# Six stream slots, 41 resident weight granules and a stream in QKV alone, in a recurrent transformer kernel

## The chip, the cores and the metric

One NeuronCore of a Trainium2 chip runs the kernel. The metric is the device time in microseconds (us) of one execution; the granted clock is that of TensorE (PE), as a share of 2.4 GHz.

## What is computed

x is (1, 2048, 1024) in bf16. With xn = layernorm(x) the result is x + A(xn) + B(xn).

```python
# A: 64 segments of 32 rows, 8 memory rows, 32 heads of 128
for s in range(64):
    h = concat([mem, xs])                  # 40 rows
    q, k, v = h @ Wq, h @ Wk, h @ Wv       # each 1024 x 4096
    p = softmax(mask(q @ k.T * scale))
    o = (p @ v) @ Wo                       # 4096 x 1024
    mem = o[:8]; outs.append(o[8:])
# B: two routed rows
r = x @ w_r; idx = two largest of r
y = (silu(x[idx] @ w_gate) * (x[idx] @ w_up)) @ w_down * sigmoid(r[idx])
B = x + scatter_add(y at idx)
```

The new memory is needed before the next segment can start, so the 64 segments run one after the other.

## The kernel before

The weights of A do not fit in SBUF. They are cut into 64 **granules** of 512 KB (128 x 2048 bf16): 48 for QKV, in six phases of eight (Q half 0, K half 0, Q half 1, K half 1, V half 0, V half 1; `PHASES`), and 16 for Wo, numbered 48 to 63. `N_RES` = 42 stay resident (`wres`, loaded at L107 in the prologue). The other 22 are fetched again in every segment, through a ring of `N_SLOT` = 4 tiles (pool `wstream`, tiles `g`): `fetch()` issues the next on SP's DMA queue (L248), `take` hands it out, and `used(g)` issues another fetch once PE has been given the matmuls of a streamed granule. So three fetches run ahead, in a fixed order. Before, the streamed granules are 16 of QKV (1, 4, 7, 10, 13, 16, 18, 21, ... 45) and six of Wo (48, 50, 53, 56, 59, 62).

The program has three parts. The **prologue** loads x, computes layernorm and writes its transposes to DRAM (`xT_d`, `zT_d`, `stl_d`), while the residents come in. The **expert stage** computes B for the two routed rows, with 46 fetches of w_gate, w_up and w_down through the same ring (L243, L245), and writes the two changed columns to `zT_d` (L318, SP's queue). The memory rows of `A_mem0` are then loaded on SP's queue (L368), transposed on PE and copied into `ST` (`mem_to_st`, L354 and L355). The **segment loop** (L374) runs, for each segment: the QKV matmuls (L505, result `PSm`); transposes of Q and K (L408); `scores(half)`, which adds the mask on PE and does the softmax on DVE and ACT over PSUM tile `SPS` (L448 max, L449 subtract, L451 exp into SBUF tile `EX`, L453 sum, then the products `PM` and `PL`); `attend` (L481, L483); the Wo projection (L545, `WO`); the output copy `OB`, and `mem_to_st` for the next segment.

The eight rows that the memory displaces in each segment ("left" rows, tile `STL`) are handled for four segments at once; with j = s mod 4, their V comes in the V phases of j=0 (L509, L530), Q in j=1, K in j=2, and their Wo projection (`WL`) in j=3. ACT's queue carries the small loads and stores (`ZT`, `ST`, `STL`, `QKL`, `qkl_d`, outputs). Order on each engine is as written; nothing reorders it.

Of the kernel before, what the change touches and what calls it, by code (L numbers as in the profile page):

```python
# [8 lines left out]
BF16 = mybir.dt.bfloat16  # L9
F32 = mybir.dt.float32  # L10
U32 = mybir.dt.uint32
ALU = mybir.AluOpType
ACTF = mybir.ActivationFunctionType
AX = mybir.AxisListType
PSUM = bass.MemoryType.PSUM
DRAM = bass.MemoryType.DRAM

N_RES = 42
N_SLOT = 4
NEG = -30000.0  # L20

PHASES = [(0, 0), (1, 0), (0, 1), (1, 1), (2, 0), (2, 1)]
# [3 lines left out]
def kernel(  # L26
# [16 lines left out]
    nc = tc.nc  # L43
    P = 128
# [3 lines left out]
    SEG = int(A_seg_len)  # L48
# [5 lines left out]
    KC = D // P  # L54
    FC = F // P
    SCALE = float(E) ** -0.5
    XM = SEG - M
    XL = M
    NK = M + SEG
# [8 lines left out]

    NG = 64
    n_str = NG - N_RES  # L70
    streamed = set(((2 * i + 1) * NG) // (2 * n_str) for i in range(n_str))

    def granule_dram(g):
        if g < 48:
# [10 lines left out]
    const = ctx.enter_context(tc.tile_pool(name="const", bufs=1))  # L85
    dram = ctx.enter_context(tc.tile_pool(name="dram", bufs=1, space=DRAM))
    wstream = ctx.enter_context(tc.tile_pool(name="wstream", bufs=N_SLOT))
    psA = ctx.enter_context(tc.tile_pool(name="psA", bufs=2, space=PSUM))
    psL = ctx.enter_context(tc.tile_pool(name="psL", bufs=1, space=PSUM))
    psT = ctx.enter_context(tc.tile_pool(name="psT", bufs=2, space=PSUM))  # L90
# [19 lines left out]
    IDENT = const.tile([P, P], BF16, name="IDENT")  # L110
    make_identity(nc, IDENT[:, :])
    MASK = const.tile([P, 2 * NK], BF16, name="MASK")
    PL = [const.tile([P, 4, 2, 32], BF16, name=f"PL{i}") for i in range(2)]
    for i in range(2):
        nc.gpsimd.memset(PL[i][:, :, :, :], 0.0)
    SPS = psS.tile([P, 4, 2, NK], F32, name="SPS")
    nc.vector.memset(SPS[:, :, :, :], 0.0)


    pc = ExitStack()  # L120
    pro = pc.enter_context(tc.tile_pool(name="pro", bufs=2))
    pro1 = pc.enter_context(tc.tile_pool(name="pro1", bufs=1))

    MF = pro1.tile([P, 2 * NK], F32, name="MF")
    nc.vector.memset(MF[:, :], 0.0)

    for q0 in range(0, P, 32):
# [3 lines left out]
    nc.vector.tensor_copy(out=MASK[:, :], in_=MF[:, :])  # L131

    RROW = wstream.tile([P, 2048], BF16, tag="g", name="RROW")[0:1, 0:S]
    WRT = pro1.tile([P, KC], BF16, name="WRT")
    nc.sync.dma_start(out=WRT[:, :], in_=B_w_r.rearrange("(k p) -> p k", p=P))
    V8 = const.tile([1, 8], F32, name="V8")
    I8 = const.tile([1, 8], U32, name="I8")
# [5 lines left out]
    def load_x(u):  # L143
        if 2 * u < NT:
            XP[u] = wstream.tile([P, 2048], BF16, tag="g", name="XP")
            nc.sync.dma_start(out=XP[u].rearrange("p (a d) -> p a d", a=2),
                              in_=x2[2 * u * P:(2 * u + 2) * P, :].rearrange("(a p) d -> p a d", a=2))
# [53 lines left out]
                          in_=Zt.rearrange("p s k r -> p s (k r)"))  # L201
        nc.sync.dma_start(out=stl_d[t][:, :], in_=L.rearrange("p k s r -> p (k s r)"))

    load_x(0)
    load_x(1)
    for t in range(NT + 4):
        if t < NT:
            if t % 2 == 1:
                load_x(t // 2 + 2)
            ST8[t] = ln_stats(pro, xt(t), P)  # L210
        if 0 <= t - 4:
            ln_e(t - 4)
        load_resident(2)
        if 0 <= t - 1 < NT:
            ln_b(t - 1)
        if 0 <= t - 2 < NT:
            ln_c(t - 2)
        if 0 <= t - 3 < NT:
            ln_d(t - 3)
# [5 lines left out]

    pc = ExitStack()
    pro = pc.enter_context(tc.tile_pool(name="prob", bufs=1))


    FH = F // 2  # L230
# [24 lines left out]

    for _ in range(N_SLOT - 1):
        fetch()
    XS = pro.tile([2, D], BF16, name="XS")
    vals = []
    for c in range(2):  # L260
# [56 lines left out]
    for c in range(2):  # L317
        nc.sync.dma_start(out=zT_d[bass.ds(vals[c] >> 5, 1), :, :, bass.ds(vals[c] & 31, 1)].rearrange("s p k r -> p (s k) r"),  # L318
                          in_=ZNEW[:, :, c:c + 1])
    pc.close()  # L320


    stp = ctx.enter_context(tc.tile_pool(name="stp", bufs=2, reuse_waits="tile"))
    one = ctx.enter_context(tc.tile_pool(name="one", bufs=1, reuse_waits="tile"))
    two = ctx.enter_context(tc.tile_pool(name="two", bufs=2, reuse_waits="tile"))

    def granule(g):
        return take("w", g) if g in streamed else res_tiles[g]

    def used(g):  # L330
        if g in streamed:
            fetch()

    def load_st(s):
        ST = stp.tile([P, KC, SEG], BF16, tag="st", name="ST")
        nc.scalar.dma_start(out=ST.rearrange("p k r -> p (k r)"), in_=xT_d[s // 4][s % 4])
        return ST

    def load_stl(g):
        STL = one.tile([P, KC, SEG], BF16, tag="stl", name="STL")  # L340
# [7 lines left out]
                                in_=qkl_d[s // 4][:, :, :, s % 4, :].rearrange("m h p c -> p (m h) c"))  # L348
        return t

    def mem_to_st(OB, ST):
        PTm = psT.tile([P, 2, P], BF16, tag="t", name="PTm")
        for c in range(2):
            nc.tensor.transpose(out=PTm[:, c, :], in_=OB[:, c * P:(c + 1) * P], identity=IDENT[:, :])  # L354
        nc.vector.tensor_copy(out=ST.rearrange("p (g c) r -> p c g r", c=2)[:, :, :, XM:SEG],  # L355
                              in_=PTm.rearrange("p c (g r) -> p c g r", g=4)[:, :, :, XM:SEG])

    def residual(PS, Zt):

        for g in range(4):  # L360
# [1 line left out]
                nc.tensor.matmul(PS[32 * g:32 * g + 32, c * P:(c + 1) * P], lhsT=Zt[:, 2 * g + c, :], rhs=IDENT[:, :],  # L362
                                 start=(c == 0), stop=False, tile_position=(0, 32 * g), skip_group_check=True)

    OB = two.tile([P, 256], BF16, tag="ob", name="OB")
    nc.vector.memset(OB[:, :], 0.0)
    for g in range(4):
        nc.sync.dma_start(out=OB[32 * g + XM:32 * g + SEG, :], in_=A_mem0[0, :, 256 * g:256 * (g + 1)])  # L368
    ST = load_st(0)
    STL = load_stl(0)  # L370
    QKL = load_qkl(0)
    mem_to_st(OB, ST)

    for s in range(NSEG):  # L374
        G, j = divmod(s, 4)
# [53 lines left out]
        def scores(half):  # L429
            if s == 0:  # L430
                for m in range(2):
                    nc.scalar.dma_start(out=QKL[:, m, half, :], in_=qkl_d[0][m, half, :, 0, :])
            q, k = QT[half], KT[half]
            nc.gpsimd.tensor_copy(out=k[:, :, 32:NK], in_=QKL[:, 1, half, :].rearrange("p (h r) -> p h r", r=XL))
            for il in range(4):
                for jq in range(4):
                    hh = 4 * il + jq
                    nc.tensor.matmul(SPS[32 * jq:32 * jq + 32, il, 0, :], lhsT=q[:, hh, :], rhs=k[:, hh, :],
                                     start=(il == 0), stop=True, tile_position=(0, 32 * jq), skip_group_check=True)
                    nc.tensor.matmul(SPS[32 * jq:32 * jq + XL, il, 1, :], lhsT=QKL[:, 0, half, hh * XL:(hh + 1) * XL],  # L440
                                     rhs=k[:, hh, :], start=False, stop=True, tile_position=(0, 32 * jq),
                                     skip_group_check=True)
            nc.tensor.matmul(SPS.rearrange("p i a k -> p i (a k)"), lhsT=IDENT[:, :],  # L443
                             rhs=MASK[:, :].unsqueeze(1).to_broadcast([P, 4, 2 * NK]),
                             start=False, stop=True, skip_group_check=True)
            S8 = SPS.rearrange("p i a k -> p (i a) k")
            NM = two.tile([P, 8], F32, tag="nm", name="NM")
            nc.vector.tensor_reduce(out=NM[:, :], in_=S8, axis=AX.X, op=ALU.max, negate=True)  # L448
            nc.vector.tensor_tensor(out=S8, in0=S8, in1=NM[:, :].unsqueeze(2).to_broadcast([P, 8, NK]), op=ALU.add)  # L449
            EX = one.tile([P, 8, NK], BF16, tag="ex", name="EX")  # L450
            nc.scalar.activation(out=EX[:, :, :], in_=S8, func=ACTF.Exp, scale=SCALE)  # L451
            DN = two.tile([P, 8], F32, tag="dn", name="DN")
            nc.vector.tensor_reduce(out=DN[:, :], in_=EX[:, :, :], axis=AX.X, op=ALU.add)  # L453
            nc.vector.reciprocal(out=DN[:, :], in_=DN[:, :])
            PM = one.tile([P, 8, 32], BF16, tag="pm", name="PM")
            PLt = PL[half].rearrange("p i a k -> p (i a) k")
            jp = (j + 3) % 4
            nc.gpsimd.memset(PLt[:, :, XL * jp:XL * (jp + 1)], 0.0)
            dnb = DN[:, :].unsqueeze(2)
            nc.vector.tensor_tensor(out=PM[:, :, :], in0=EX[:, :, 0:32], in1=dnb.to_broadcast([P, 8, 32]), op=ALU.mult)  # L460
            nc.vector.tensor_tensor(out=PLt[:, :, XL * j:XL * (j + 1)], in0=EX[:, :, 32:NK],
                                    in1=dnb.to_broadcast([P, 8, XL]), op=ALU.mult)
            PTm = two.tile([P, 4, 64], BF16, tag="ptm", name="PTM")
            PTl = two.tile([P, 4, 64], BF16, tag="ptl", name="PTL")
            nc.vector.transpose(out=PTm.rearrange("p i q -> p (i q)"), in_=PM.rearrange("p b k -> p (b k)"))
            nc.vector.transpose(out=PTl.rearrange("p i q -> p (i q)"), in_=PLt.rearrange("p b k -> p (b k)"))
            PTs[half] = (PTm, PTl)
            if half == 1 and s + 1 < NSEG:
                nxt["qkl"] = load_qkl(s + 1)

        def attend(half, ph):
            if half not in OT:
                OT[half] = two.tile([P, 4, 4, SEG], BF16, tag="ot", name="OT")
            PTm, PTl = PTs[half]
            OP = psO.tile([P, 2, 512], F32, tag="otp", name="OP")
            for il in range(4):
# [102 lines left out]
        for w, Gv in late[4:]:  # L579
            project(WL, w, Gv, lhs_left, w == late[-1][0])  # L580
        if j == 3:
            OL = one.tile([P, 256], BF16, tag="ol", name="OL")
            nc.scalar.copy(out=OL[:, :], in_=WL[:, 0:256])
            o4 = out2[4 * G * SEG:4 * (G + 1) * SEG, :].rearrange("(s r) d -> s r d", s=4)
            for g in range(4):
                nc.scalar.dma_start(out=o4[:, XM:SEG, 256 * g:256 * (g + 1)], in_=OL[32 * g:32 * (g + 1), :])
# [37 lines left out]
```

## Time and profile before

| | |
|---|---|
| runs | median 2810.72 us of 3 (2807.4 to 2813.32) |
| the profiled execution | 2811.76 us, its span 2810.0 us, mean granted clock 0.864 |
| busy share of the span | PE 69%, PE weight loads 36%, DVE 26%, ACT 16%, POOL 4% |
| chain that ended last | DMA 47%, PE 22%, issue 19%, DVE 7% |
| HBM read over the span | 804.28 MB |

The busy shares are averages over the three parts. The chain follows the work back from the last instruction; "issue" in it is time in which an engine waited for nothing that the profile shows. A wait is put down to what ended it. DMA share is the mean busy share of the core's 16 DMA engines; GB/s is what they moved.

### The profile page before, as it was taken

What the parts mean: (1) busy time and instruction counts of PE and PEld (TensorE: products, weight loads), DVE (VectorE), ACT (ScalarE), POOL (GpSimd) and SP (SyncE); (2) the same over time, 40 slices, a digit from 0 to 9 for tenths busy, and PEclk for the clock granted to TensorE, in tenths of its full rate; (3) what the DMA queues carried; (4) which work ended last, traced back from release to release, by engine and by line L of the source; (5) the groups of instructions that cost most, each with busy time, mean ns of one, the idle gap of its engine ahead of it and who ended that gap; (6) DMA issues with size and microseconds to landing.
All of it is one profiled execution on the core that took longest, in us unless ns stands there. A gap on an engine that the chain in (4) does not pass through costs nothing.

```text
span 2810.0 us, 82148 instructions
## 1 busy us (share of the span) xinstructions
PE 1949.7 (69%) x36873; PEld 998.7 (36%) x36873; DVE 722.0 (26%) x2021; ACT 459.1 (16%) x1017; POOL 112.9 (4%) x436
## 2 busy tenths in 40 slices
PE   3356777677777777767776777777677777777776
PEld 3222333333334333333333333333333333333333
DVE  4301222222222222222222222212222222222222
ACT  3201111111111111111111111111111111111111
POOL 4100000000000000000000000000000000000000
PEclk9668888889898898888988888988988888888888
DMA  9975988989898998979988898988889897988987
GB/s 299 318 265 179 311 299 293 300 279 336 292 318 300 310 316 275 312 268 319 298 301 300 279 306 286 317 302 300 295 298 314 280 318 268 309 301 293 316 304 264
DMA packets 367877, 831.69 MB, mean 296 GB/s; under 512 B 68482, under 2 KB 121762, under 8 KB 367524
## 3 DMA queue, kind: packets, MB, share of 16 engines
q1 hardware_dynamic: 292212, 796.00, 82.7%
q10 hardware_dynamic: 75312, 30.44, 4.0%
q8 instruction: 288, 4.72, 0.7%
q14 instruction: 65, 0.53, 0.1%
HBM read 804.28 MB, written 22.02 MB: 294 GB/s over the span
## 4 chain that ended last, share of the span: by engine, by line
DMA 47%; PE 22%; issue 19%; DVE 7%; ACT 2%; ACTq 1%; POOL 1%; SPq 1%; POOLq 0%; DVEq 0%
DMA g<-in_A_Wq_dram 14%; DMA g<-in_A_Wo_dram 13%; PE PSm L505 10%; DMA g<-in_A_Wv_dram 7%; DMA g<-in_A_Wk_dram 5%; PE WO L545 4%; DMA out_dram<-OB 2%; PE PSl L509 2%; DMA zT_d<-Tz 1%; PE PTq L408 1%; DMA qkl_d<-QS 1%; DVE SPS L449 1%; DVE NM L448 1%; ACT EX L451 1%; DVE DN L453 1%
## 5 line engine op out<-in xcount | busy, mean ns | idle before, releaser
L505 PE MATMUL PSm<-wres,ST 128*32 128x512 bf16 x8192 | 806.3, 436 | 14.7 <-DVE ST L355 13.9
L505 PE MATMUL PSm<-g,ST 128*32 128x512 bf16 x4096 | 454.0, 432 | 333.8 <-DMA g<-in_A_Wq_dram 186.8
L505 PEld LDWEIGHTS <-ST 128*32 128x32 bf16 x12288 | 332.1, 102 | 790.3 <-issue 459.6
L545 PEld LDWEIGHTS <-OT 128*32 128x32 bf16 x8192 | 233.7, 107 | 178.9 <-issue 153.6
L509 PE MATMUL PSl<-wres,STL 128*32 128x512 bf16 x2048 | 233.5, 443 | 50.3 <-DVE VL L530 47.0
L545 PE MATMUL WO<-g,OT 128*32 128x256 bf16 x3072 | 178.0, 313 | 121.6 <-DMA g<-in_A_Wo_dram 120.4
L517 ACT CAST XB<-PSm 128x512 bf16<-128x512 f32 x256 | 149.5, 584 | 654.9 <-PE PSm L505 475.5
L545 PE MATMUL WO<-wres,OT 128*32 128x256 bf16 x5120 | 254.3, 305 | 0.0
L486 ACT CAST OT<-OP 128x256 bf16<-128x256 f32 x256 | 95.2, 372 | 481.7 <-PE OP L483 481.7
L488 DVE CAST OTL<-OP 128x64 bf16<-128x64 f32 x256 | 57.5, 225 | 402.1 <-ACT OT L486 402.1
L408 PE MATMUL PTq<-IDENT,XB 128*128 128x128 bf16 x1024 | 108.4, 232 | 74.8 <-ACT XB L517 73.0
L448 DVE TENSOR_REDUCE NM<-SPS 128x8 f32<-128x320 f32 x128 | 62.9, 492 | 366.3 <-PE SPS L443 366.3
L451 ACT ACTIVATE EX<-SPS 128x320 bf16<-128x320 f32 x128 | 55.9, 437 | 612.1 <-DVE SPS L449 576.6
L509 PEld LDWEIGHTS <-STL 128*32 128x32 bf16 x3072 | 93.7, 107 | 143.9 <-issue 101.6
L416 DVE COPY KT<-PTq 128x512 bf16<-128x512 bf16 x128 | 54.3, 425 | 332.0 <-PE PTq L408 330.8
L408 PEld LDWEIGHTS <-XB 128*128 128x128 bf16 x1024 | 61.8, 102 | 203.0 <-ACT XB L517 172.2
L481 PE MATMUL OP<-PTM,VM 32*128 32x40 bf16 x2048 | 102.0, 186 | 42.5 <-DVE VM L527 38.2
L413 DVE COPY QT<-PTq 128x512 bf16<-128x512 bf16 x128 | 52.2, 408 | 272.6 <-PE PTq L408 272.6
L481 PEld LDWEIGHTS <-VM 32*128 32x128 bf16 x2048 | 70.1, 95 | 142.9 <-issue 92.9
L509 PE MATMUL PSl<-g,STL 128*32 128x512 bf16 x1024 | 113.9, 431 | 7.1 <-DVE XBl L521 7.1
L398 POOL COPY ZL<-ZT 128x64 bf16<-128x64 bf16 x64 | 15.1, 236 | 2424.7 <-DMA ZT<-zT_d 2246.7
L483 PE MATMUL OP<-PTL,VL 32*128 32x40 bf16 x2048 | 98.1, 182 | 0.0
(98 smaller groups left out, 1562.9 us busy)
## 6 DMA issues: line engine op xcount, KB each, us to landing
g<-in_A_Wq_dram SPq DMA_DIRECT2D x384, 512.0 KB
g<-in_A_Wo_dram SPq DMA_DIRECT2D x384, 512.0 KB
g<-in_A_Wk_dram SPq DMA_DIRECT2D x320, 512.0 KB
g<-in_A_Wv_dram SPq DMA_DIRECT2D x320, 512.0 KB
qkl_d<-QS ACTq DMA_DIRECT2D x64, 128.0 KB
QKL<-qkl_d ACTq DMA_DIRECT2D x63, 128.0 KB
g<-in_B_w_gate_dram SPq DMA_DIRECT2D x16, 448.0 KB
g<-in_B_w_up_dram SPq DMA_DIRECT2D x16, 448.0 KB
```

Source lines behind the costliest of these rows:

```text
L408: nc.tensor.transpose(out=PTq[:, il, :, :].rearrange("p j r -> p (j r)"), in_=XB[:, il * P:(il + 1) * P], identity=IDENT[:, :])
L416: nc.vector.tensor_copy(out=KT[half][:, :, 0:32], in_=pv)
L448: nc.vector.tensor_reduce(out=NM[:, :], in_=S8, axis=AX.X, op=ALU.max, negate=True)
L451: nc.scalar.activation(out=EX[:, :, :], in_=S8, func=ACTF.Exp, scale=SCALE)
L481: nc.tensor.matmul(o, lhsT=VM[q0:q0 + 32, c0:c0 + P], rhs=PTm[q0:q0 + 32, il, 0:NK], start=True, stop=False, tile_position=(q0, 0), skip_g ...
L483: nc.tensor.matmul(o, lhsT=VL[q0:q0 + 32, c0:c0 + P], rhs=PTl[q0:q0 + 32, il, 0:NK], start=False, stop=True, tile_position=(q0, 0), skip_g ...
L486: nc.scalar.copy(out=OT[half][:, 2 * ph:2 * ph + 2, :, :], in_=ov[:, :, :, 0:SEG])
L488: nc.vector.tensor_copy(out=OTL[:, h0:h0 + 8, j, :].rearrange("p (a i) r -> p a i r", a=2), in_=ov[:, :, :, SEG:NK])
L505: nc.tensor.matmul(PSm[32 * jq:32 * jq + 32, :], lhsT=ST[:, kc, :], rhs=Gv[:, 512 * jq:512 * (jq + 1)], start=(kc == 0), stop=(kc == KC - ...
L509: nc.tensor.matmul(PSl[32 * jq:32 * jq + 32, :], lhsT=STL[:, kc, :], rhs=Gv[:, 512 * jq:512 * (jq + 1)], start=(kc == 0), stop=(kc == KC - 1),
L517: nc.scalar.copy(out=XB[:, :], in_=PSm[:, :])
L545: nc.tensor.matmul(PS[32 * g:32 * g + 32, 0:256], lhsT=lhs(h), rhs=Gv[:, D * hs + 256 * g:D * hs + 256 * (g + 1)], start=False, stop=(last ...
```

## The change

- `N_SLOT` goes from 4 to 6 and `N_RES` from 42 to 41. The 23 streamed granules are spread over the first 48 granules only: 1, 3, 5, ... 21, 24, 26, ... 46. No Wo granule is streamed, so in j=3 all 16 `WL` projections are "late": four before `mem_to_st`, twelve after.
- The memory rows are loaded on ACT's queue ahead of the expert stage, and `ST` of segment 0 is made there too.
- Working tiles share buffers: `OT` with `QT` and `KT`, `PT2` of half 1 with `XB`, `OL` with `OB`, `MF` with a stream slot; `PL` lies in pool `one`. x is loaded three pairs ahead in place of two.
- The exponential is written back to `SPS` in PSUM; sum and products read it there.

```diff
-N_RES = 42
-N_SLOT = 4
+N_RES = 41
+N_SLOT = 6
...
-    streamed = set(((2 * i + 1) * NG) // (2 * n_str) for i in range(n_str))
+    streamed = set(((2 * i + 1) * 48) // (2 * n_str) for i in range(n_str))
...
-    load_x(0)
-    load_x(1)
+    for u in range(3):
+        load_x(u)
...
+    OB = pro.tile([P, 256], BF16, name="MEM0")
+    nc.vector.memset(OB[:, :], 0.0)
+    for g in range(4):
+        nc.scalar.dma_start(out=OB[32 * g + XM:32 * g + SEG, :], in_=A_mem0[0, :, 256 * g:256 * (g + 1)])
...
+    ST = load_st(0)
+    mem_to_st(OB, ST)
...
-    OB = two.tile([P, 256], BF16, tag="ob", name="OB")
-    nc.vector.memset(OB[:, :], 0.0)
-    for g in range(4):
-        nc.sync.dma_start(out=OB[32 * g + XM:32 * g + SEG, :], in_=A_mem0[0, :, 256 * g:256 * (g + 1)])
-    ST = load_st(0)
     STL = load_stl(0)
     QKL = load_qkl(0)
-    mem_to_st(OB, ST)
...
-            EX = one.tile([P, 8, NK], BF16, tag="ex", name="EX")
-            nc.scalar.activation(out=EX[:, :, :], in_=S8, func=ACTF.Exp, scale=SCALE)
+            nc.scalar.activation(out=S8, in_=S8, func=ACTF.Exp, scale=SCALE)
...
-            nc.vector.tensor_reduce(out=DN[:, :], in_=EX[:, :, :], axis=AX.X, op=ALU.add)
+            nc.vector.tensor_reduce(out=DN[:, :], in_=S8, axis=AX.X, op=ALU.add)
...
-            PTm = two.tile([P, 4, 64], BF16, tag="ptm", name="PTM")
-            PTl = two.tile([P, 4, 64], BF16, tag="ptl", name="PTL")
+            PT2 = one.tile([P, 2, 4, 64], BF16, tag="pt", name="PT2") if half == 0 else \
+                two.tile([P, 2, 4, 64], BF16, tag="xb", name="PT2")
+            PTm, PTl = PT2[:, 0], PT2[:, 1]
...
-                OT[half] = two.tile([P, 4, 4, SEG], BF16, tag="ot", name="OT")
+                OT[half] = one.tile([P, 4, 4, SEG], BF16, tag=("qt", "kt")[half], name="OT")
...
-            OL = one.tile([P, 256], BF16, tag="ol", name="OL")
+            OL = two.tile([P, 256], BF16, tag="ob", name="OL")
```

SP's queue between Q half 1 of one segment and K half 0 of the next, before (`g` is a tile of the ring):

```order
L248 DMA g<-in_A_Wq_dram 128x2048 x3
L248 DMA g<-in_A_Wk_dram 128x2048 x3
L248 DMA g<-in_A_Wv_dram 128x2048 x5
L248 DMA g<-in_A_Wo_dram 128x2x1024 x6
L248 DMA g<-in_A_Wq_dram 128x2048 x3
L248 DMA g<-in_A_Wk_dram 128x2048 x2
```

and after:

```order
L249 DMA g<-in_A_Wq_dram 128x2048 x3
L249 DMA g<-in_A_Wk_dram 128x2048 x4
L249 DMA g<-in_A_Wv_dram 128x2048 x8
L249 DMA g<-in_A_Wq_dram 128x2048 x4
L249 DMA g<-in_A_Wk_dram 128x2048 x4
```

The six Wo rows are gone, and seven more fetches stand in the QKV phases, three of them in V.

SP's queue behind the expert stage's last fetch, before (`ZNEW` holds the two changed columns):

```order
L318 DMA zT_d<-ZNEW 1024x1x1
L318 ISA
L318 REGISTER_ALU
L318 ISA
L318 DMA zT_d<-ZNEW 1024x1x1
L368 DMA OB<-in_A_mem_dram 8x256 x4
L248 DMA g<-in_A_Wk_dram 128x2048
```

and after:

```order
L333 DMA zT_d<-ZNEW 1024x1x1
L333 ISA
L333 REGISTER_ALU
L333 ISA
L333 DMA zT_d<-ZNEW 1024x1x1
L249 DMA g<-in_A_Wk_dram 128x2048 x2
```

The four loads of the memory rows no longer stand behind the two writes.

PE from the last transposes of the expert stage to the first matmul of the loop, before (`RNEW` holds the two changed rows):

```order
L314 LDWEIGHTS RNEW
L314 MATMUL PZ<-IDENT,RNEW 128x2
L354 LDWEIGHTS OB
L354 MATMUL PTm<-IDENT,OB 128x128
L354 LDWEIGHTS OB
L354 MATMUL PTm<-IDENT,OB 128x128
L505 LDWEIGHTS ST
L505 MATMUL PSm<-wres_207,ST 32x512
```

After, the two transposes of the memory rows stand ahead of the expert stage's first PE work:

```order
L267 LDWEIGHTS MEM_1142
L267 MATMUL PTm<-IDENT,MEM_1142 128x128
L267 LDWEIGHTS MEM_1142
L267 MATMUL PTm<-IDENT,MEM_1142 128x128
L284 LDWEIGHTS SIGR
L284 MATMUL PSG<-ONE_1187,SIGR 2x1
```

With them gone, the first L505 follows the last transpose of `RNEW` directly.

## Rows read from the trace of the kernel before

**Rows 1.** Head of the page: the span on core 0.

```profile
span 2810.0 us, 82148 instructions
```

**Rows 2.** Waits of the whole span: engine, form <- releaser: us, count, longest us.

```profile
PE PSm L505 <- DMA g<-in_A_Wq_dram: 186.8, 185, 3.0
PE WO L545 <- DMA g<-in_A_Wo_dram: 120.4, 165, 3.4
PE PSm L505 <- DMA g<-in_A_Wv_dram: 107.2, 102, 3.4
```

**Rows 3.** Windows: stretch us, busy by engine (x), granted clock, DMA share, GB/s.

```profile
110.00:118.00 8.00, 0.16 (x1) 0.07 (x1) 0.66 (x3) 2.77 (x3) 0.00 (x0) 0.50 1.00 386
140.00:160.00 20.00, 7.51 (x204) 6.37 (x202) 0.00 (x0) 0.00 (x0) 0.00 (x0) 0.50 0.96 336
118.30:122.30 4.00, 0.77 (x24) 0.79 (x25) 2.02 (x7) 2.42 (x3) 0.00 (x0) 0.50 0.03 13
1161.50:1181.10 19.60, 14.18 (x279) 7.16 (x282) 7.94 (x23) 3.42 (x8) 0.38 (x2) 0.85 0.96 321
1223.20:1226.20 3.00, 3.00 (x120) 2.48 (x116) 0.98 (x3) 1.20 (x4) 0.00 (x0) 1.00 0.61 200
1229.20:1232.60 3.40, 2.74 (x42) 1.53 (x34) 0.48 (x2) 0.27 (x1) 0.00 (x0) 0.50 1.03 408
1275.00:1305.00 30.00, 23.08 (x396) 10.32 (x399) 10.17 (x27) 5.66 (x12) 1.08 (x6) 0.93 0.93 308
270.50:2803.50 2533.00, 1826.23 (x35282) 922.19 (x35282) 651.55 (x1853) 401.97 (x924) 68.30 (x378) 0.87 0.88 300
```

**Rows 4.** DMA from 400 to 2700 us: queue: packets, MB, share.

```profile
DMA packets 291154, 688.16 MB, mean 299 GB/s; under 512 B 56025, under 2 KB 86764, under 8 KB 290849
q1 hardware_dynamic: 224123, 656.71, 83.1%
```

**Rows 5.** PE timeline: start us, us, operation [idle before]; loop's start and end.

```profile
190.36 0.35 PE L314 MATMUL PZ<-IDENT,RNEW 2*128 2x2 bf16 x8 [2.62 <-DVE RNEW L310]
199.86 0.37 PE L354 MATMUL PTm<-IDENT,OB 128*128 128x128 bf16 x2 [9.15 <-DMA OB<-in_A_mem_dram]
200.51 0.62 PE L505 MATMUL PSm<-wres,ST 128*32 128x512 bf16 x4 [0.28 <-DVE ST L355]
...
270.56 0.62 PE L505 MATMUL PSm<-wres,ST 128*32 128x512 bf16 x4 [0.28 <-DVE ST L355]
...
2800.92 2.54 PE L545 MATMUL WL<-wres,OTL 128*32 128x256 bf16 x80
```

**Rows 6.** PE timeline, a j=0 segment: granules 33, 46, Wo 59, next 1.

```profile
1209.01 0.40 PE L505 MATMUL PSm<-g,ST 128*32 128x512 bf16 x4 [1.57 <-DMA g<-in_A_Wv_dram]
...
1222.29 0.40 PE L505 MATMUL PSm<-wres,ST 128*32 128x512 bf16 x4
...
1228.99 0.62 PE L545 MATMUL WO<-g,OT 128*32 128x256 bf16 x8 [2.28 <-DMA g<-in_A_Wo_dram]
...
1233.45 0.64 PE L505 MATMUL PSm<-g,ST 128*32 128x512 bf16 x4
```

**Rows 7.** PE timeline, a j=3 segment: granule 46, two Wo stops, next 1.

```profile
1177.84 1.04 PE L505 MATMUL PSm<-wres,ST 128*32 128x512 bf16 x8
...
1184.81 0.40 PE L545 MATMUL WO<-g,OT 128*32 128x256 bf16 x8 [0.24 <-DMA g<-in_A_Wo_dram]
...
1186.56 0.40 PE L545 MATMUL WO<-g,OT 128*32 128x256 bf16 x8 [0.43 <-DMA g<-in_A_Wo_dram]
...
1189.95 0.39 PE L505 MATMUL PSm<-g,ST 128*32 128x512 bf16 x4
```

**Rows 8.** Chain that ended last, 118 to 136 us: start us, us, what.

```profile
122.44 3.57 DMA g<-in_B_w_gate_dram
```

**Rows 9.** Groups of DVE instructions: busy, mean ns, idle before.

```profile
L448 DVE TENSOR_REDUCE NM<-SPS 128x8 f32<-128x320 f32 x128 | 62.9, 492 | 366.3 <-PE SPS L443 366.3
L453 DVE TENSOR_REDUCE DN<-EX 128x8 f32<-128x320 bf16 x128 | 62.2, 486 | 75.9 <-ACT EX L451 75.9
```

More of the change, by code (lines that the diff above doesn't have):

```diff
@@ L87 @@
     wstream = ctx.enter_context(tc.tile_pool(name="wstream", bufs=N_SLOT))
+    stp = ctx.enter_context(tc.tile_pool(name="stp", bufs=2))
     psA = ctx.enter_context(tc.tile_pool(name="psA", bufs=2, space=PSUM))
@@ L112 @@
     MASK = const.tile([P, 2 * NK], BF16, name="MASK")
-    PL = [const.tile([P, 4, 2, 32], BF16, name=f"PL{i}") for i in range(2)]
-    for i in range(2):
-        nc.gpsimd.memset(PL[i][:, :, :, :], 0.0)
     SPS = psS.tile([P, 4, 2, NK], F32, name="SPS")
@@ L121 @@
     pro = pc.enter_context(tc.tile_pool(name="pro", bufs=2))
-    pro1 = pc.enter_context(tc.tile_pool(name="pro1", bufs=1))
-    MF = pro1.tile([P, 2 * NK], F32, name="MF")
+    MF = wstream.tile([P, 2 * NK], F32, tag="g", name="MF")
     nc.vector.memset(MF[:, :], 0.0)
@@ L133 @@
     RROW = wstream.tile([P, 2048], BF16, tag="g", name="RROW")[0:1, 0:S]
-    WRT = pro1.tile([P, KC], BF16, name="WRT")
+    WRT = const.tile([P, KC], BF16, name="WRT")
     nc.sync.dma_start(out=WRT[:, :], in_=B_w_r.rearrange("(k p) -> p k", p=P))
@@ L208 @@
             if t % 2 == 1:
-                load_x(t // 2 + 2)
+                load_x(t // 2 + 3)
             ST8[t] = ln_stats(pro, xt(t), P)
@@ L257, with load_st, mem_to_st @@
         fetch()
+    def load_st(s):
+        ST = stp.tile([P, KC, SEG], BF16, tag="st", name="ST")
+        nc.scalar.dma_start(out=ST.rearrange("p k r -> p (k r)"), in_=xT_d[s // 4][s % 4])
+        return ST
+    def mem_to_st(OB, ST):
+        PTm = psT.tile([P, 2, P], BF16, tag="t", name="PTm")
+        for c in range(2):
+            nc.tensor.transpose(out=PTm[:, c, :], in_=OB[:, c * P:(c + 1) * P], identity=IDENT[:, :])
+        nc.vector.tensor_copy(out=ST.rearrange("p (g c) r -> p c g r", c=2)[:, :, :, XM:SEG],
+                              in_=PTm.rearrange("p c (g r) -> p c g r", g=4)[:, :, :, XM:SEG])
+    ST = load_st(0)
+    mem_to_st(OB, ST)
     XS = pro.tile([2, D], BF16, name="XS")
@@ L320 @@
     pc.close()
-    stp = ctx.enter_context(tc.tile_pool(name="stp", bufs=2, reuse_waits="tile"))
     one = ctx.enter_context(tc.tile_pool(name="one", bufs=1, reuse_waits="tile"))
     two = ctx.enter_context(tc.tile_pool(name="two", bufs=2, reuse_waits="tile"))
+    PL = [one.tile([P, 4, 2, 32], BF16, name=f"PL{i}") for i in range(2)]
+    for i in range(2):
+        nc.gpsimd.memset(PL[i][:, :, :, :], 0.0)
     def granule(g):
@@ L332, in used @@
             fetch()
[L334 to L337, printed above, removed]
     def load_stl(g):
@@ L349, in load_qkl @@
         return t
[L351 to L356, printed above, removed]
     def residual(PS, Zt):
@@ L459, in scores @@
             dnb = DN[:, :].unsqueeze(2)
-            nc.vector.tensor_tensor(out=PM[:, :, :], in0=EX[:, :, 0:32], in1=dnb.to_broadcast([P, 8, 32]), op=ALU.mult)
-            nc.vector.tensor_tensor(out=PLt[:, :, XL * j:XL * (j + 1)], in0=EX[:, :, 32:NK],
+            nc.vector.tensor_tensor(out=PM[:, :, :], in0=S8[:, :, 0:32], in1=dnb.to_broadcast([P, 8, 32]), op=ALU.mult)
+            nc.vector.tensor_tensor(out=PLt[:, :, XL * j:XL * (j + 1)], in0=S8[:, :, 32:NK],
                                     in1=dnb.to_broadcast([P, 8, XL]), op=ALU.mult)
-            PTm = two.tile([P, 4, 64], BF16, tag="ptm", name="PTM")
-            PTl = two.tile([P, 4, 64], BF16, tag="ptl", name="PTL")
+            PT2 = one.tile([P, 2, 4, 64], BF16, tag="pt", name="PT2") if half == 0 else \
+                two.tile([P, 2, 4, 64], BF16, tag="xb", name="PT2")
+            PTm, PTl = PT2[:, 0], PT2[:, 1]
             nc.vector.transpose(out=PTm.rearrange("p i q -> p (i q)"), in_=PM.rearrange("p b k -> p (b k)"))
```

## The prediction

> **What bounds the kernel now.** I read the page's head first: one core, a span of 2810.0 us in an execution of 2811.76 us [rows 1]. Then the table of waits: the three largest groups of PE waits on a streamed granule add up to 186.8 + 120.4 + 107.2 = 414.4 us [rows 2], 6.5 us for each of 64 segments; 120.4 of it lies in the output projection, the rest in QKV.
>
> The windows tell whether this is a lack of rate or of slots [rows 3]. In the whole loop DMA is busy for 0.88 of the time at 300 GB/s; in the QKV phases of a j=3 segment 0.96 at 321 GB/s. So there the stream itself is nearly full; what is missing lies elsewhere. The stream queue q1 carries 656.71 of 688.16 MB [rows 4], a share of 0.954; at 321 GB/s one granule of 0.5243 MB therefore lands every 0.5243 / (0.954 x 0.321) = **1.71 us**. I call this spacing p.
>
> Before, a segment takes (2800.92 + 2.54 - 270.56) / 63 = 40.2 us [rows 5], the first, longer one left out.
>
> **The loop after the change.** A segment now streams 23 granules in place of 22, all in QKV (1, 3, ... 46), and none in Wo. I follow the PE from the moment it takes granule 1 (time 0) to granule 1 of the next segment.
>
> (a) With six slots, five fetches run ahead. Between granule 46 and the next granule 1 PE takes nothing from the stream, and the six slots fill at their own pace (6 x 1.71 = 10.3 us). Without waits this stretch lasts 1233.45 - 1222.29 - 2.28 = 8.88 us in a j=0 segment [rows 6], and I take that for j=0, 1 and 2; after a j=3 segment 1189.95 - 1177.84 - 0.24 - 0.43 = 11.44 us [rows 7]. The 2.28, 0.24 and 0.43 are the waits on streamed Wo in these rows, which the change removes.
>
> (b) The slot of granule 1 is free after its 0.40 us on PE [rows 6], and a transfer with nothing ahead of it takes 3.57 us from issue to landing [rows 8]: the 7th granule lands at 4.0 us, little after the six before it.
>
> (c) Sixteen more follow at p, if PE takes each at once: granule 46 lands at 4.0 + 16 x 1.71 = 31.4 us.
>
> (d) The cycle is 31.4 + 8.88 = 40.2 us for j=1 and j=2, and 31.4 + 11.44 = 42.8 us for j=3. For j=0 the V phases hold twice the PE work (the displaced rows): the first V granule, the 16th of the stream, lands at 4.0 + 9 x 1.71 = 19.4 us, and from the first streamed V to the next granule 1 PE needs 1233.45 - 1209.01 - 2.28 = 22.2 us [rows 6], together 41.6 us. The mean is (41.6 + 2 x 40.2 + 42.8) / 4 = **41.2 us**, 1.0 more than before, times 63 = **+63 us**.
>
> The price p is the unknown: no row shows six loop granules in flight. Its lower bound is 0.5243 / (0.954 x 0.408) = 1.35 us, from 3.4 us in a Wo phase after the stream had stood; 0.386 gives 1.42 us (seven or eight transfers in flight, PE nearly idle), and 0.5243 / 0.336 = 1.56 us is the expert stage, with four slots and no other queue at work. The upper bound, from the QKV phases of a j=2 segment with displaced K rows, is 0.5243 / (0.954 x 0.308) = 1.78 us [rows 3]. I take 1.71, since its row is the same phases with the same other traffic and DMA was busy for 0.96 of it, which seems to leave more slots 4% to fill. Each 0.1 us of p costs (9 + 3 x 16) / 4 x 0.1 = 1.43 us a segment, 90 us in all.
>
> **The start.** The memory rows came over SP's queue behind the two writes of zT_d, and PE stood from 190.71 (190.36 + 0.35) to 200.51, 9.15 of it put down to that load [rows 5]. They now come over ACT's queue before the expert stage and the two transposes go with them; SP keeps the two zT_d writes but has four fewer DMAs behind them. Taken: -9.7 us (200.51 - 190.71 = 9.80, less 0.1 for issue). The other end is 0, if a first-segment tile that reuses the expert stage's memory waits for those writes instead. Before the expert stage DMA is busy for 0.03 of 4 us while the routed rows are prepared [rows 3]; two more gate fetches of 0.459 MB now run there: -2 x 0.459 / 0.336 = -2.7 us (other end 0). One resident less: -0.524 / 0.386 = -1.4 us [rows 3] (other end 0, if the layer norm sets the end). Four small ACT-queue loads and x loaded one pair earlier are hidden by that same resident stream. Sum -13.8 us. The first segment stays as it is.
>
> **What I cost at nothing.** Softmax in PSUM: the sum over 320 f32 elements from PSUM takes about what the same reduction of bf16 from SBUF takes now (492 against 486 ns [rows 9]); SPS is held through sum and products too, but the next scores come 16 granules later. Bounds +-0.1 us a segment; cover: PE works on V meanwhile. Shared buffers: OT takes QT's and KT's buffer after the scores that read them, PT2 of half 1 that of an XB already transposed, OL that of an OB long sent; PE's own order covers each. In j=3, six projections of displaced rows move from before the memory transposes to after them, on the same engine: the sum is the same. SP's queue only holds fetches in the loop, so a fetch that waits delays none but fetches.
>
> **Sum.** 2811.76 + 63 - 13.8 = 2861 us for the profiled execution. The median of the runs stands 1.0 us below it, so the forecast is **2860 us**.
>
> **The rivals.**
>
> *A, six in flight raise the rate* (faster). If p falls to 1.56: j=0 takes 18.0 + 22.2 = 40.2, j=1 and 2 4.0 + 25.0 + 8.9 = 37.8, j=3 40.4, mean 39.1; (39.1 - 40.2) x 63 - 14 = -83 us, **2727 us**. It decides below p = 1.66, where the loop costs the 14 us that the start gives. For it: 386 GB/s with more transfers in flight and 408 in a Wo phase [rows 3], both with DMA busy throughout, while 0.96 stood beside 321 GB/s: a busy share near 1 is not yet the full rate. Against: the 408 was a burst, and the QKV phases carry the writes of ACT's queue besides. At p = 1.42 the mean would be 37.1 us and the time 2600 us. The Trainium skill's page "DMA: Bandwidth & Descriptors", section "Anatomy of one DMA", says that a transfer costs about 2.0 us plus its bytes over 436 GB/s and that the fixed part is mostly waiting for completion; what only waits can be covered by more transfers in flight, which speaks for A. By its fit a lone granule takes an estimated 3.2 us, against 3.57 us in the row for a gate transfer, which is smaller [rows 8]. The same page's section "Specifications" gives the core some 358 GB/s of HBM, by which p would be an estimated 1.54 us and the time some 2710 us; as a ceiling the 386 GB/s of this trace disagree with it.
>
> *B, the QKV phases fall to the lower rate* (slower still). The stream is denser there, and every write of ACT's queue meets it. At p = 1.78: 42.2, 41.4, 41.4 and 43.9, mean 42.2; +126 - 14, **2923 us**. For it: 308 GB/s in j=2. Against: that row also holds PE-side stops.
>
> *C, Wo without stops shortens the gap.* After the 2.28 us stop a matmul group takes 0.62 to 0.64 us where it took 0.40 before [rows 6]: the granted clock is 0.50 there, 1.2 GHz, and 1.00 before the stop [rows 3]. If that goes with the stop, about 1 us falls away in three of four segments: -47 us, **2813 us**, about no change. Against: PE then waits in QKV, and the clock may fall there as well.
>
> *D, the change doesn't reach the loop* (the streams' place doesn't matter, the bytes do): 23 granules in place of 22 at 300 GB/s in all give 40.2 x (0.954 x 23/22 + 0.046) = 42.0 us, which is near B.
>
> **How the numbers follow.** My forecast has 0.46, A 0.32, B with D 0.13, C 0.09. A measurement tells a change from none at about 0.2%, some 6 us. The forecast's own range, p from 1.66 to 1.76, is 2815 to 2905. The range of 8 in 10 takes in A at 1.56 and B without the start's gain: **2725 to 2940**. Faster by over 0.2%: A and a little of C, 0.35. Within 0.2%: most of C, 0.06. Slower: 0.59.
>
> **What would show it.** Right: no wait on Wo granules any more; the DMA share falling towards the end of each Wo phase; the PE's waits gathered in phases Q to V, most in the V phases; about 306 GB/s of stream there; the first segment starting near 187 us; the 9.15 us wait gone. Wrong: a QKV stretch at 335 GB/s or more (A), at 308 or less (B), a stretch from granule 46 to granule 1 well under 8.9 us (C), or a first segment that still starts near 196 us or later.

## The result, and the profile after

The changed kernel takes **2714.95 us** (median of 4 runs, 2711.71 to 2721.07) beside 2809.06 us before, a ratio of 0.9666 with a 95% interval of 0.9644 to 0.9688. It is 94 us faster; 2860 us was forecast, slower by 49, and the range began at 2725. The profiled execution took 2711.71 us.

The page of the changed kernel: the span, the busy times, the DMA packets and the chain's shares by engine.

```profile
span 2709.7 us, 82405 instructions
PE 1950.0 (72%) x36873; PEld 984.4 (36%) x36873; DVE 721.0 (27%) x2021; ACT 458.4 (17%) x1017; POOL 116.7 (4%) x436
...
DMA packets 328567, 864.74 MB, mean 319 GB/s; under 512 B 69490, under 2 KB 122770, under 8 KB 328212
...
DMA 42%; PE 25%; issue 24%; DVE 5%; ACT 2%; ACTq 1%; SPq 1%; POOL 1%; POOLq 0%; DVEq 0%
```

The same two lines of the kernel before:

```profile
PE 1949.7 (69%) x36873; PEld 998.7 (36%) x36873; DVE 722.0 (26%) x2021; ACT 459.1 (16%) x1017; POOL 112.9 (4%) x436
...
DMA packets 367877, 831.69 MB, mean 296 GB/s; under 512 B 68482, under 2 KB 121762, under 8 KB 367524
```

PE is busy for the same time as before, and more bytes (864.74 MB, against 831.69) came in less time. So time went from waits. The waits of PE, as in [rows 2]:

```profile
PE PSm L505 <- DMA g<-in_A_Wv_dram: 176.4, 264, 2.8
PE PSm L505 <- DMA g<-in_A_Wk_dram: 139.4, 163, 3.6
PE PSm L505 <- DMA g<-in_A_Wq_dram: 101.5, 136, 2.2
PE PTq L408 <- ACT XB L517: 54.3, 82, 2.0
PE SPS L438 <- POOL KT L434: 47.4, 17, 5.6
PE PSl L509 <- DVE VL L530: 42.8, 16, 3.1
```

The Wo wait (120.4 us) is gone, and the waits on weights lie in QKV, the largest share in V, as forecast. All waits on streamed granules of A add up to 417.3 us; before, with the one on Wk that [rows 2] do not have, they were 450.7:

```profile
PE PSm L505 <- DMA g<-in_A_Wk_dram: 36.3, 61, 1.9
```

So they fell by 33 us in all. Windows of the changed kernel, columns as in [rows 3]: two of the prologue, one of the expert stage, the QKV phases of a j=3 segment, a j=0 segment from granule 46 to the next segment's first, and the loop.

```profile
0.00:40.00 40.00, 15.87 (x141) 13.04 (x142) 22.13 (x55) 17.54 (x27) 19.48 (x30) 0.91 0.97 360
40.00:80.00 40.00, 24.15 (x215) 19.59 (x211) 22.78 (x59) 20.76 (x33) 20.46 (x19) 0.55 1.07 365
116.00:136.00 20.00, 9.03 (x238) 7.68 (x238) 0.00 (x0) 0.00 (x0) 0.00 (x0) 0.50 1.03 406
1261.00:1281.40 20.40, 14.38 (x226) 5.51 (x225) 7.52 (x21) 2.81 (x7) 1.15 (x6) 0.79 1.02 384
1325.20:1332.30 7.10, 6.35 (x196) 4.62 (x198) 1.91 (x7) 2.03 (x6) 0.00 (x0) 1.00 0.53 186
300.00:2580.00 2280.00, 1690.92 (x32676) 842.25 (x32676) 601.68 (x1712) 372.02 (x856) 66.57 (x348) 0.87 0.88 322
```

The same of the kernel before, where [rows 3] have no row:

```profile
0.00:40.00 40.00, 16.20 (x135) 13.28 (x136) 21.57 (x54) 15.23 (x24) 17.95 (x31) 1.00 0.86 298
40.00:80.00 40.00, 17.29 (x148) 14.60 (x146) 16.21 (x42) 16.42 (x26) 15.34 (x13) 1.00 1.02 311
1222.30:1233.40 11.10, 8.13 (x200) 5.26 (x198) 1.92 (x7) 2.03 (x6) 0.00 (x0) 0.80 0.81 299
```

QKV of j=3 runs at 384 GB/s in place of 321, the expert stage at 406 in place of 336, the prologue at 360 in place of 298. PE at the start of the loop, as in [rows 5]:

```profile
165.95 0.35 PE L329 MATMUL PZ<-IDENT,RNEW 2*128 2x2 bf16 x8 [2.62 <-DVE RNEW L325]
166.23 0.40 PE L505 MATMUL PSm<-wres,ST 128*32 128x512 bf16 x4
169.35 0.62 PE L509 MATMUL PSl<-wres,STL 128*32 128x512 bf16 x4 [2.72 <-DMA STL<-stl_d]
```

The 9.15 us wait is gone, and the loop starts at 166.2 us in place of 200.5.

Where the time went, from the starts of the stages on PE in both traces (us):

| stage | before | after | difference |
|---|---|---|---|
| start to the first expert transposes (PXS) | 121.3 | 108.6 | -12.7 |
| expert stage, to the end of PZ | 69.4 | 57.7 | -11.7 |
| PZ to the first L505 | 9.8 | 0.0 | -9.8 |
| first segment | 70.0 | 75.3 | +5.3 |
| 63 segments | 63 x 40.20 | 63 x 39.09 | -70 |

The sum is -99, beside -100 between the two profiled executions.

### The profile page after: what moved, and what is told of

Its sections match the earlier page's. It is cut to its first block, busy times and chain, and to the rows that moved or that the text cites. A ratio compares the mean times of both kernels' runs of the same rounds, so it can differ in the third digit from the quotient of the medians.

```text
span 2709.7 us, 82405 instructions
## 1 busy us (share of the span) xinstructions
PE 1950.0 (72%) x36873; PEld 984.4 (36%) x36873; DVE 721.0 (27%) x2021; ACT 458.4 (17%) x1017; POOL 116.7 (4%) x436
## 2 busy tenths in 40 slices
DMA packets 328567, 864.74 MB, mean 319 GB/s; under 512 B 69490, under 2 KB 122770, under 8 KB 328212
## 4 chain that ended last, share of the span: by engine, by line
DMA 42%; PE 25%; issue 24%; DVE 5%; ACT 2%; ACTq 1%; SPq 1%; POOL 1%; POOLq 0%; DVEq 0%
DMA g<-in_A_Wv_dram 18%; DMA g<-in_A_Wq_dram 11%; PE PSm L505 10%; PE WO L545 8%; DMA g<-in_A_Wk_dram 5%; PE WL L545 2%; DMA zT_d<-Tz 1%; PE OP L481 1%; DMA out_dram<-OL 1%; DMA qkl_d<-QS 1%; PE PSl L509 1%; DMA ST<-xT_d 1%; DMA QKL<-qkl_d 1%; PE PTq L408 1%; PE OP L483 1%
## 5 line engine op out<-in xcount | busy, mean ns | idle before, releaser
L505 PE MATMUL PSm<-g,ST 128*32 128x512 bf16 x5888 | 667.9, 440 | 422.3 <-DMA g<-in_A_Wv_dram 176.4
L505 PE MATMUL PSm<-wres,ST 128*32 128x512 bf16 x6400 | 724.8, 444 | 14.4 <-DVE ST L268 13.6
L505 PEld LDWEIGHTS <-ST 128*32 128x32 bf16 x12288 | 337.9, 101 | 934.3 <-issue 555.6
L545 PE MATMUL WO<-wres,OT 128*32 128x256 bf16 x8192 | 295.3, 294 | 13.9 <-issue 13.8
L545 PEld LDWEIGHTS <-OT 128*32 128x32 bf16 x8192 | 222.4, 105 | 39.0 <-issue 20.0
L509 PE MATMUL PSl<-g,STL 128*32 128x512 bf16 x1472 | 161.5, 424 | 49.9 <-DVE VL L530 42.8
L509 PE MATMUL PSl<-wres,STL 128*32 128x512 bf16 x1600 | 176.8, 429 | 9.0 <-DVE XBl L521 6.3
L450 ACT ACTIVATE SPS<-SPS 128x320 f32<-128x320 f32 x128 | 54.0, 422 | 638.5 <-DVE SPS L449 542.8
L509 PEld LDWEIGHTS <-STL 128*32 128x32 bf16 x3072 | 91.2, 104 | 132.8 <-issue 87.9
L481 PEld LDWEIGHTS <-VM 32*128 32x128 bf16 x2048 | 69.1, 96 | 119.3 <-issue 105.4
L481 PE MATMUL OP<-PT,VM 32*128 32x40 bf16 x2048 | 99.2, 187 | 12.5 <-DVE VM L527 11.8
L483 PE MATMUL OP<-PT,VL 32*128 32x40 bf16 x2048 | 95.5, 183 | 0.4 <-issue 0.4
L521 DVE CAST XBl<-PSl 128x512 bf16<-128x512 f32 x64 | 43.6, 681 | 171.1 <-PE PSl L509 152.5
```

The lines of the kernel that those rows point to most:

```text
L450: nc.scalar.activation(out=S8, in_=S8, func=ACTF.Exp, scale=SCALE)
L481: nc.tensor.matmul(o, lhsT=VM[q0:q0 + 32, c0:c0 + P], rhs=PTm[q0:q0 + 32, il, 0:NK], start=True, stop=False, tile_position=(q0, 0), skip_g ...
L483: nc.tensor.matmul(o, lhsT=VL[q0:q0 + 32, c0:c0 + P], rhs=PTl[q0:q0 + 32, il, 0:NK], start=False, stop=True, tile_position=(q0, 0), skip_g ...
L505: nc.tensor.matmul(PSm[32 * jq:32 * jq + 32, :], lhsT=ST[:, kc, :], rhs=Gv[:, 512 * jq:512 * (jq + 1)], start=(kc == 0), stop=(kc == KC - ...
L509: nc.tensor.matmul(PSl[32 * jq:32 * jq + 32, :], lhsT=STL[:, kc, :], rhs=Gv[:, 512 * jq:512 * (jq + 1)], start=(kc == 0), stop=(kc == KC - 1),
L545: nc.tensor.matmul(PS[32 * g:32 * g + 32, 0:256], lhsT=lhs(h), rhs=Gv[:, D * hs + 256 * g:D * hs + 256 * (g + 1)], start=False, stop=(last ...
```

## The experiments

Theory D: more slots in flight raise the stream's rate, and that is the gain. Theory W, its rival: the gain is the Wo phase without stops. First the slots alone, then the spread alone, in both kernels.

**Four slots** in the changed kernel:

```diff
-N_SLOT = 6
+N_SLOT = 4
...
-    for u in range(3):
+    for u in range(2):
...
-                load_x(t // 2 + 3)
+                load_x(t // 2 + 2)
```

> The changed kernel with four stream slots in place of six (and x loaded two pairs ahead, since a third does not fit the ring). Theory D (six slots raise the stream's rate, and that is the gain): the expert stage goes back from about 404 to about 336 GB/s and from 57.7 to about 69 us, the prologue to about 121 us, and a segment takes 43 to 45 us (four slots refill in the Wo phase, the fifth granule lands 4.0 us after granule 1, 18 more at 1.71 us, 8.4 us to the next granule 1): 2950 to 3090 us. Theory W (the gain is the Wo phase without stops, the slots matter little): the segments stay at 39 to 40 us and the time at 2730 to 2780 us.

3097.99 us, ratio 1.1059 (1.0980 to 1.1138), 44.9 us a segment: theory D, 8 us over its range. The waits on streamed granules are 656.7 us here, against 417.3 with six slots:

```profile
PE PSm L505 <- DMA g<-in_A_Wk_dram: 366.0, 357, 3.7
PE PSm L505 <- DMA g<-in_A_Wv_dram: 247.2, 278, 3.1
PE PSm L505 <- DMA g<-in_A_Wq_dram: 43.5, 81, 2.0
```

The size of the packets is not the cause: Wo granules come in packets of 2 KB and QKV granules of 4 KB, and this run streams QKV granules alone, as the changed kernel does.

**Five slots** (`N_SLOT = 5` alone):

> The changed kernel with five slots. Theory D: between four and six, a segment of 40 to 42 us, 2780 to 2880 us, the expert stage at 370 to 390 GB/s. Theory W: within 20 us of the changed kernel.

2821.06 us, 1.0048 (1.0009 to 1.0087), 40.7 us a segment. The expert stage and the loop with four slots, then with five:

```profile
128.00:148.00 20.00, 7.27 (x195) 6.13 (x193) 0.00 (x0) 0.00 (x0) 0.00 (x0) 1.00 0.93 327
400.00:2600.00 2200.00, 1586.25 (x27342) 743.79 (x27338) 508.17 (x1440) 312.78 (x719) 55.67 (x294) 0.77 0.81 280
```

```profile
122.00:138.00 16.00, 7.21 (x193) 6.06 (x190) 0.00 (x0) 0.00 (x0) 0.00 (x0) 0.50 1.02 396
400.00:2600.00 2200.00, 1599.36 (x30303) 785.94 (x30306) 561.12 (x1593) 347.14 (x797) 62.40 (x324) 0.85 0.86 309
```

327, 396 and 406 GB/s with four, five and six slots, in the same code: D holds, and most of the rate comes with the fifth (396 is above the 370 to 390 that I expected).

**The old spread in the changed kernel**, and **the new spread in the kernel before**:

```diff
-    streamed = set(((2 * i + 1) * 48) // (2 * n_str) for i in range(n_str))
+    streamed = set(((2 * i + 1) * NG) // (2 * n_str) for i in range(n_str))
```

> The changed kernel with its 23 streamed granules spread over all 64 again (17 in QKV, 6 in Wo), six slots and 41 residents kept. Theory D: the spread costs, as the slots already hold what Wo would need; with it undone the stops in Wo are short and a segment takes 36.5 to 38.5 us, 2560 to 2680 us. Theory W: the stops in Wo come back (2.4 us of Wo phase in each segment, at the lower granted clock), QKV gives back 1.3 us: about 40.2 us a segment, 2780 us.

2644.83 us, 0.9450 (0.9381 to 0.9518), 38.0 us a segment: faster than the change by some 2%, as theory D has it.

The same line turned round, in the kernel before:

> The kernel before with its 22 streamed granules in QKV alone, four slots and 42 residents kept. Theory D: with four slots the spread is a loss, since only four granules are fetched in the Wo phase; a segment of 41.5 to 43.5 us, 2890 to 3020 us. Theory W: the Wo phase falls from 9.9 to 7.5 us as in the changed kernel and a segment to about 39 us, 2730 to 2760 us.

3032.96 us, 1.0825 (1.0738 to 1.0911), 43.8 us a segment: theory D again, 13 us over its range. So the spread is a loss with four slots and with six, and W falls as the cause of the gain. Its Wo phase does shrink (from 9.5 to 5.9 us in j=0), but QKV grows by more (32.0 to 39.0). PE's waits there, in the kernel before with the new spread:

```profile
PE PSm L505 <- DMA g<-in_A_Wk_dram: 367.2, 318, 3.5
PE PSm L505 <- DMA g<-in_A_Wv_dram: 199.2, 250, 3.2
```

By segment the change can be cut into three steps, each between two kernels that were run: spread 40.20 to 43.83 (+3.6); one resident less, together with shared buffers, softmax in PSUM and the memory rows, 43.83 to 44.93 (+1.1); two more slots 44.93 to 39.09 (-5.8). The prices hold for this order alone: with the spread as the last step, all the rest takes a segment from 40.20 to 38.03 (-2.2) and the spread from there to 39.09 (+1.1). With six slots the new spread costs less than a third of what it costs with four. What the resident costs by itself was not run.

**The smaller parts.** x loaded two pairs ahead, six slots kept (the last two pieces of the first diff):

> The changed kernel with x loaded two pairs ahead again, six slots kept. Theory S (the prologue is shorter since more ring slots let SP's queue go on to the residents): the first expert transposes stay at 107 to 110 us. Theory L (it is the third pair loaded ahead): they go back towards 114 to 121 us and the whole by 5 to 12 us.

PXS starts at 110.0 us, the whole takes 2721.79 us (one run). With four slots it started at 119.4 to 123.0 us in all four kernels, with six at 105.4 to 112.0; so the prologue's gain belongs to the slots, as theory S has it; this run and the one with four slots (119.4) differ in nothing else. Five slots gave 113.8 to 123.8, which leaves that case open.

The exponential in an SBUF tile again:

```diff
+            EX = one.tile([P, 8, NK], BF16, tag="ex", name="EX")
-            nc.scalar.activation(out=S8, in_=S8, func=ACTF.Exp, scale=SCALE)
+            nc.scalar.activation(out=EX[:, :, :], in_=S8, func=ACTF.Exp, scale=SCALE)
...
```

with `EX` in place of `S8` in the sum and the products.

> The changed kernel with the exponential written to a bf16 tile in SBUF again and sum and products read from there. Theory D: the softmax's place costs nothing; within 0.3% of the changed kernel (2707 to 2723 us). Rival: PSUM reads and the longer hold on SPS cost 0.2 us or more a segment; 13 us faster or more.

2729.02 us, 0.9717 (0.9659 to 0.9774). Run again beside the changed kernel on one chip:

> The changed kernel with the exponential in an SBUF tile again, a second time beside the changed kernel on one chip. The softmax's place costs nothing: within 0.3% of it. Rival: the form in PSUM is the faster by 0.3% or more, as the first run left possible.

> The changed kernel itself, as the measure for the other runs on this chip: 0.965 to 0.969 of the kernel before, 39.1 us a segment.

2734.44 us, 0.9738 (0.9679 to 0.9798), against 2711.44 us, 0.9678 (0.9620 to 0.9737). "Within 0.3%" missed twice: the SBUF form was slower by 14 and 23 us. The intervals of the ratios overlap, but on the one chip each of its four runs (2724.68 to 2747.44) is slower than each of the changed kernel's four (2708.29 to 2720.08). The instructions are alike (changed kernel, groups of DVE):

```profile
L452 DVE TENSOR_REDUCE DN<-SPS 128x8 f32<-128x320 f32 x128 | 62.8, 491 | 71.7 <-ACT SPS L450 71.7
L459 DVE TENSOR_TENSOR PM<-SPS,DN 128x256 bf16<-128x256 f32 x128 | 54.3, 424 | 4.4
```

491 and 424 ns, against 486 and 425 from SBUF. That PSUM costs nothing is shown. That the form in PSUM gains some 0.5 to 0.9% is likely; how stays open.

The memory rows alone, in the kernel before:

```diff
+    OB = pro.tile([P, 256], BF16, name="MEM0")
...
+        nc.scalar.dma_start(out=OB[32 * g + XM:32 * g + SEG, :], in_=A_mem0[0, :, 256 * g:256 * (g + 1)])
...
+    ST = load_st(0)
+    mem_to_st(OB, ST)
```

> The kernel before with the memory rows loaded on ACT's queue and ST of segment 0 made ahead of the expert stage, nothing else. The prediction's term: PE goes from the last transposes of the expert stage to the first matmul of the loop without the 9.8 us gap, and the loop starts 9 to 10 us earlier; the first segment takes 70 us as before, or up to 3 us more if STL then comes late. The whole 2796 to 2804 us beside 2810.

2801.92 us (one run). The first L505 starts 0.3 us after the last transposes begin, so the 9.8 us gap is gone, but the first segment takes 73.9 us in place of 70.0, a little more than the 3 us that I allowed: some 6 us are left of the gap's 9.8.

**Towards a better kernel.** Five slots, 42 residents, 22 granules spread over all 64:

> The changed kernel with five slots, 42 residents and its 22 streamed granules spread over all 64. If the fifth slot gives most of the rate (1.42 to 1.55 us a granule in j=2 and j=3 with five slots, 1.38 to 1.48 with six) and a granule less saves what it costs, it is level with the six-slot kernel spread over 64: 2620 to 2670 us. If the sixth slot is worth more than the resident: 2680 to 2740 us.

2632.76 us, 0.9372 (0.9317 to 0.9428), 37.5 us a segment: level with six slots spread the same way. Then the residual tile earlier, since PE waited for POOL there:

```diff
-        hook(1, 4, fetch_z)
+        hook(0, 3, fetch_z)
```

> Six slots, 41 residents, 23 granules spread over all 64, and the residual tile ZT fetched in the first phase (after granule 3) in place of the second (after granule 12). In the run spread over 64 PE waited 97.8 us for POOL's KT copy, which stands behind the copy of ZT on POOL. If ZT's late landing is what POOL waits for, most of that goes: 30 to 70 us off that run, 2570 to 2615 us. If POOL waits for QKL, nothing changes: 2630 to 2655 us.

2604.98 us, 0.9294 (0.9239 to 0.9350). The wait, in the run spread over 64 and then in this one:

```profile
PE SPS L438 <- POOL KT L434: 97.8, 30, 5.7
```

```profile
PE SPS L438 <- POOL KT L434: 27.1, 12, 5.8
```

> The same early ZT in the kernel with five slots, 42 residents and 22 granules spread over all 64. If ZT is the cause: 2560 to 2605 us; if not, 2620 to 2645 us as without it.

2598.22 us, 0.9260 (0.9187 to 0.9334). Both beat the changed kernel by some 4%; between the two the intervals don't decide.

## Why the prediction was wrong

- **The step that failed is p.** "I take 1.71, since its row is the same phases with the same other traffic and DMA was busy for 0.96 of it, which seems to leave more slots 4% to fill." 1.71 is about right for four slots: from granule 13 to 46, over the segments of each j, a granule landed every 1.74 to 1.78 us in the changed kernel with four (bytes of q1 over time). With five it was 1.42 to 1.59 and with six 1.52, 1.63, 1.48 and 1.38 us for j=0 to 3. The share of 0.96 did not mean what I read into it (last section). My own rows held the warning, 386 and 408 GB/s at a busy share near 1, and I gave them to rival A at 0.32. The "seven or eight transfers in flight" of the row at 386 were too many: by the times of issue and the bytes of q1, about five still had bytes to come (2.4 MB at 111 us), as many as six slots let run ahead. So its p of 1.42 was the nearest row, and I passed it over.
- **The structure (a) to (d) holds with four slots and is too short with six.** With four it says 4.0 + 18 x 1.74 = 35.3 us from granule 1 to 46; measured in j=1 to 3, 35.6 to 35.9. With six and the measured p, 27.7 in j=2 and 26.1 in j=3; measured 29.1 and 27.9, since the 7th granule came at 4.4 to 4.6 us and PE did not take each one behind it at once. Over the four j the structure with the measured p gives 38.2 us a segment in place of 41.2, rival C takes off 0.9, and 39.1 was measured: so p is worth -3.0, and stops of PE that the structure has at nothing took 1.8 back. That the spread costs was right.
- **Rival A came true** with its 2727 us, partly by luck: it has 40.2, 37.8, 37.8 and 40.4 us for j=0 to 3, and 40.5, 40.0, 37.0 and 39.1 were measured. In j=1 "if PE takes each at once" fails, PE waiting for POOL's KT for 2.2 us a segment.
- **Rival C came true too**: from granule 46 to the next granule 1 the four j take 7.3, 8.2, 7.8 and 11.1 us where I had 8.88, 8.88, 8.88 and 11.44, and in the window from 1325.2 us the granted clock is 1.00, 2.4 GHz, where it was 0.80 before. These 0.9 us a segment are in the -70.
- **The start** was -13.8 by three terms; -34.2 was measured. The memory rows came as priced (-9.8). The expert stage gave 11.7 and not 2.7, since all its fetches came faster: p again, in a stage in which I did not apply it. The prologue gave 12.7 and not 1.4; the slots did that too, but whether by a faster stream or by letting SP's queue go on to the residents sooner, these runs do not tell apart. "The first segment stays as it is" was wrong by 5.3 us: 2.72 of it is the wait for STL above, behind which the L509 stand; more comes from XBl (13.4 us of waits against 10.4).
- Of what I cost at nothing, the softmax in PSUM cost nothing. The shared buffers were not tried by themselves; they stand in the step of +1.1 us above.

The Trainium skill, page "DMA: Bandwidth & Descriptors", section "Anatomy of one DMA", says that the fixed cost of a transfer is mostly completion latency; its fit is for transfers that gpsimd issues, and these are on SP's queue. That more transfers in flight cover this time was my own step, in rival A. The rates of 327, 396 and 406 GB/s go the way it says, but no run here shows that it is the completion that they cover. Its 358 GB/s in "Specifications" is exceeded by 406 here, with one core at work.

## What to carry to other kernels

A DMA busy share near 1 is not the full rate: compare the GB/s of stretches that have more transfers in flight at the same share before calling a stream full. Price the slots in every stage that uses the ring, not only in the loop. A bundle of edits can win by one and lose by another: here two more slots gave 5.8 us a segment beside the new spread, while the spread, the lost resident and the rest had taken 4.7, and the version without the new spread is the faster. What one edit is worth depends on the others that are in: the spread cost 3.6 us with four slots and 1.1 with six.

## What the runs showed of the hardware that I had not expected

With four slots the DMA engines were busy for 0.93 of the expert stage at 327 GB/s, with six for 1.03 at 406. The share rose by some 11%, the rate by 24%. The packet records of q1 in these windows hold the rest: a packet of 3584 bytes took 140 ns at the median with four, five and six slots alike, but packets of over 300 ns were 3.9%, 1.2% and 0.4% of all, and the mean 161, 147 and 144 ns. Long packets count as busy and move no more bytes.

In the loop, from granule 13 to 46 of j=3 segments, packets of 4 KB go the same way: a median of 159 ns in all three, over 300 ns 5.7%, 2.6% and 2.1%, and a mean of 188, 171 and 168 ns. But with six slots and the old spread 5.1% are long in the like stretch (granule 12 to 45), at a mean of 178 ns, so the number of slots alone does not set them. What makes packets long was not tried and stays open.
